# Attention, gated unit and soft mixture on one core: another order in the first pair of heads, the last slice by halves, normalisers and idle products moved

## The chip, the cores and the metric

The kernel runs on one core of one Trainium2 chip. A core has a matrix engine (TensorE, PE in the profile, with its weight loads as PEld), VectorE (DVE), ScalarE (ACT), GpSimd (POOL) and a queue for transfers (SyncE, SP). Each engine works through its own list of instructions in order; semaphores hold it where data are missing. The metric is the time of one execution on the device in microseconds, the median of several runs.

## The reference

```python
def _attn_ref(q, k, v):                       # q, k, v: 4 x 8 x 1152 x 64
    q_pool = q.reshape(B, H, S // 2, 2, D).mean(axis=3)
    scores = 1.0 / np.sqrt(D) * np.matmul(q_pool, k.transpose(0, 1, 3, 2))
    scores = scores - np.max(scores, axis=-1, keepdims=True)
    attn = np.exp(scores)
    attn = attn / (np.sum(attn, axis=-1, keepdims=True) + 1e-09)
    return np.matmul(attn, v)
def _moe_ref(x, w_gate, w_val, w_out):        # x: 2304 x 512, d_ff 1536
    g = x @ w_gate
    silu = g * (1.0 / (1.0 + np.exp(-g)))
    return silu * (x @ w_val) @ w_out
def _moe2_ref(x, phi, w1, w2):                # 8 experts of 4 slots
    logits = x @ phi
    d = np.exp(logits - logits.max(0, keepdims=True))
    d /= d.sum(0, keepdims=True) + 1e-09
    slot_input = (d.T @ x).reshape(E, S_per_e, D)
    for e in range(E):
        slot_out[e] = np.maximum(slot_input[e] @ w1[e], 0.0) @ w2[e]
    c = np.exp(logits - logits.max(1, keepdims=True))
    c /= c.sum(1, keepdims=True) + 1e-09
    return c @ slot_out.reshape(n_slots, D)
```

The pooled attention gives 4 x 576 tokens of 512 numbers; the gated unit (`_moe_ref`) works on them, and the soft mixture on its result.

## The kernel before

The work is written as one Python program; a scheduler with a timeline orders it per engine. What it keeps to: the program's order, priorities (`tc.high_priority`), the data, and the hand-made order marks `after` and `not_before`, which put an instruction behind a named one, or behind the last (or an earlier) exponential written so far.

*Attention* runs in 16 steps, one for each batch and pair of heads. Every number of 32 bits is split into a high and a low half of 16 bits, and products are made of the halves. `load_pair` loads a pair's keys, queries and values (`kr`, `qr`, `vr`); `split_pair` adds the two queries of a pool (`qr`, line 241), casts keys and queries to 16 bits (`kh`, `qh`), subtracts for the low halves (`kl`, `ql`), and copies the halves by transfers into the layouts that TensorE wants (`KK`, `QQ`, `KL`, `QH`, and `QD` for the maxima). The first pair has loads of its own for its first head (`first_split`).

Each pair's row maxima are computed one pair ahead: `row_max` multiplies `QD` and `kh` (`mx`, line 340) into a bank of PSUM, and VectorE reduces it (`mp`, lines 346 and 355; gathered in `nm`, line 358). The negated maxima go as a row `mt` by a transfer into `QH` (line 364), so that the second product of a score (`st`, line 421, "low score") subtracts the maximum. The first pair's own maxima come from `row_max_first` (products at line 291, reductions from line 301 on), head by head, the second head's while the first head's scores run.

A unit of a pair is one bank of scores: products at lines 420 and 421, the exponential on ScalarE (`P`, line 426), its low half `PL` on GpSimd (line 433), and later the products with V (`pv`). There are 21 units in a pair. Small constants are made in `selections`, at unit 20 of the program's first pair, on GpSimd: the identity in 16 bits `id16`, and the selection matrices `SEL`, `SELW` and `CN`.

*The gated unit* runs over 9 blocks of 256 tokens, each in 6 slices: products `g` and `v` (lines 691 to 696), tanh on ScalarE (line 702), two operations on VectorE (lines 703 and 705, the second multiplies by `v`), a cast to 16 bits (line 723), the low half (line 725), products for the mixture's logits `lp` (lines 735 and 740), which VectorE adds to `La` (line 746), and a transposing transfer. It fills the time from the fifth pair on.

*The mixture's end.* `block_end` gives a block's logits `L` (line 765), the running maximum, its correction `al` and the exponential `dT` (line 790); `block_turned` transposes it (`dt`, line 805) into `dS`, and `G` sums the tokens by slot. Behind the last `L` stand 30 products `warm` whose result nobody reads (line 771). `normalisers` turn the sums into factors `rn`, today folded into `CN`. After the last block `gt`, `si4p`, `siTp` and `hp` follow each other to the slots' inputs and the experts.

## Time and profile before

| | before |
|---|---|
| median of 3 runs | 897.52 us (895.04 to 897.69) |
| the profiled execution | 888.35 us, of it the span 886.6 |
| mean granted clock of TensorE | 0.973 |
| TensorE busy | 826.4 us |
| VectorE, ScalarE, GpSimd busy | 550.0, 366.3, 457.9 us |

The span is the time from the first to the last instruction of one profiled execution. A granted clock of 1.00 is 2.4 GHz, 0.50 is 1.2 GHz. In a row of a timeline the first number is the start in us, the second the length, then engine, line, operation, what it writes and reads, and in brackets the idle time of the engine before it and what ended it.

### The profile page before, as it was taken

The page shows a single profiled execution, that of the slowest core. Times are in us where ns is not written, and L with a number is a line of the kernel's source. Part 1 is how long each engine was busy: PE and PEld are TensorE (multiplying, and loading weights), DVE is VectorE, ACT ScalarE, POOL GpSimd, SP SyncE. Part 2 cuts the span into 40 slices and gives each one's busy share as a digit, 9 for nine tenths or more (in the row PEclk, how much of TensorE's full clock was granted, in tenths as well). Part 3 has the DMA queues.
Part 4 walks back from the last instruction along what each step waited for, and adds up shares of the span by engine and source line. Part 5 has one row for each costly group of instructions (what it writes and reads, how often), then busy time and mean ns, then how long its engine had stood idle before and what let it go on. Part 6 is the DMA issues. An engine that isn't in the chain of part 4 may idle for free.

```text
span 886.6 us, 23761 instructions
## 1 busy us (share of the span) xinstructions
PE 826.4 (93%) x9954; PEld 586.8 (66%) x9954; DVE 550.0 (62%) x1056; ACT 366.3 (41%) x690; POOL 457.9 (52%) x403
## 2 busy tenths in 40 slices
PE   5878898999888899999999999999999999997997
PEld 2545565677665567777776777777677777775445
DVE  5768777549787747585767767775744444444223
ACT  4545668578584633333333333333333212212112
POOL 8968669477888953655566365547345200000100
PEclk9989899899999989999999999999999999998998
DMA  6663847859588861454434171514112398457899
GB/s 193 172 163 79 264 134 218 244 152 264 138 246 226 230 173 25 102 108 97 101 81 118 32 177 32 120 30 85 33 25 37 113 307 271 84 164 189 283 280 287
DMA packets 154267, 134.69 MB, mean 152 GB/s; under 512 B 83632, under 2 KB 123120, under 8 KB 154160
## 3 DMA queue, kind: packets, MB, share of 16 engines
q1 hardware_dynamic: 152000, 133.13, 56.4%
q8 instruction: 78, 1.28, 0.6%
q10 hardware_dynamic: 2160, 0.04, 0.1%
q14 instruction: 29, 0.24, 0.1%
HBM read 84.10 MB, written 7.86 MB: 104 GB/s over the span
## 4 chain that ended last, share of the span: by engine, by line
PE 71%; DMA 11%; DVE 10%; issue 2%; SPq 2%; POOL 2%; ACT 2%; DVEq 0%; ACTq 0%; POOLq 0%
PE st L421 6%; PE st L420 6%; PE mx L340 5%; PE g L691 5%; PE g L696 5%; PE g L695 5%; PE v L691 5%; PE v L696 5%; PE v L695 4%; DMA qr<-in_qT 3%; PE pv L464 3%; PE pv L465 3%; PE pv L466 3%; DVE mp L346 3%; PE pv L456 2%
## 5 line engine op out<-in xcount | busy, mean ns | idle before, releaser
L433 POOL TENSOR_TENSOR PL<-P 128x512 f16<-128x512 f32 (+1 forms) x311 | 338.0, 1099 | 209.3 <-ACT P L426 205.8
L426 ACT ACTIVATE P<-st 128x512 f32<-128x512 f32 (+1 forms) x336 | 190.6, 580 | 249.2 <-PE st L421 205.8
L346 DVE TENSOR_REDUCE mp<-mx 128x1 f32<-128x512 f32 x270 | 179.0, 682 | 42.9 <-PE mx L340 41.3
L420 PE MATMUL st<-QQ,KK 128*128 128x512 f16 (+1 forms) x576 | 147.2, 292 | 6.4 <-ACT P L426 6.0
L421 PE MATMUL st<-QH,KL 65*128 65x512 f16 (+1 forms) x576 | 147.8, 295 | 4.6 <-DMA QH<-mt 2.8
L465 PE MATMUL pv<-VV,P 128*128 128x64 f16 x1088 | 141.2, 196 | 0.0
L464 PE MATMUL pv<-VV,P 128*128 128x65 f16 x1088 | 140.4, 195 | 0.5 <-DVE x L496 0.4
L466 PE MATMUL pv<-VV,PL 128*128 128x65 f16 x1088 | 139.0, 194 | 0.3 <-POOL PL L433 0.2
L691 PE MATMUL g<-xT,wgv 128*128 128x256 f16 x432 | 119.2, 276 | 4.1 <-DVE hs L703 3.4
L340 PE MATMUL mx<-kh,QD 128*128 128x512 f16 x270 | 105.5, 407 | 16.7 <-DVE mp L346 8.0
L464 PEld LDWEIGHTS <-P 128*128 128x128 bf16 x1088 | 105.7, 100 | 22.3 <-DVE x L496 3.4
L696 PE MATMUL g<-xT,wgv 128*128 128x256 f16 x432 | 119.0, 276 | 0.0
L695 PE MATMUL g<-xT,wgv 128*128 128x256 f16 x432 | 119.0, 275 | 0.0
L466 PEld LDWEIGHTS <-PL 128*128 128x128 f16 x1088 | 105.1, 100 | 20.7 <-issue 8.9
L696 PE MATMUL v<-xT,wgv 128*128 128x256 f16 x432 | 118.0, 273 | 0.0
L691 PE MATMUL v<-xT,wgv 128*128 128x256 f16 x432 | 118.0, 273 | 0.0
L695 PE MATMUL v<-xT,wgv 128*128 128x256 f16 x432 | 117.9, 273 | 0.0
L465 PEld LDWEIGHTS <-P 128*128 128x128 bf16 x1088 | 104.6, 99 | 10.3 <-issue 1.5
L691 PEld LDWEIGHTS <-wgv 128*128 128x128 f16 x864 | 85.3, 99 | 20.2 <-issue 2.7
L695 PEld LDWEIGHTS <-wgv 128*128 128x128 f16 x864 | 85.1, 98 | 17.4 <-issue 3.9
L696 PEld LDWEIGHTS <-wgv 128*128 128x128 f16 x864 | 85.1, 99 | 17.1 <-issue 0.8
L421 PEld LDWEIGHTS <-KL 65*128 65x128 f16 x576 | 52.1, 99 | 34.3 <-issue 13.2
(181 smaller groups left out, 1215.7 us busy)
## 6 DMA issues: line engine op xcount, KB each, us to landing
w<-in_w SPq DMA_DIRECT2D x16, 1024.0 KB, 7.4
w<-in_w SPq DMA_DIRECT2D x64, 256.0 KB, 5.5
vr<-in_vP SPq DMA_DIRECT2D x16, 585.0 KB, 5.3
KK<-kh SPq DMA_DIRECT2D x62, 144.0 KB, 2.9
qr<-in_qT SPq DMA_DIRECT2D x15, 576.0 KB, 4.8
kr<-in_kT SPq DMA_DIRECT2D x15, 576.0 KB, 4.4
r<-in_w_out SPq DMA_DIRECT2D x12, 512.0 KB, 4.4
r<-in_w_gate SPq DMA_DIRECT2D x24, 256.0 KB, 5.5
```

Of the source, the lines that this page charges most:

```text
L340: nc.tensor.matmul(t, q, kh[:, k0:k0 + kw], start=True, stop=True)
L346: nc.vector.reduce_max(out=mp[:, g, c:c + 1], in_=t, axis=AX.X)
L420: nc.tensor.matmul(t[:, o:o + w], KK[:, k], QQ[:, q0:q0 + w], start=True, stop=False)
L421: nc.tensor.matmul(t[:, o:o + w], KL[:, k], QH[:, q0:q0 + w], start=False, stop=True)
L426: marks.append(nc.scalar.activation(P32[:, :o], t[:, :o], AF.Exp, scale=1.0 / 16.0).ins.name)
L433: eng.tensor_tensor(out=PL[:, :o], in0=P32[:, :o], in1=PH[:, :o], op=ALU.subtract)
L464: nc.tensor.matmul(dst[:, :D + 1], PH[:, q], VV[:, c, 0, :], start=first, stop=False, skip_group_check=True)
L465: nc.tensor.matmul(dst[:, :D], PH[:, q], VV[:, c, 1, :D], start=False, stop=False, skip_group_check=True)
L466: nc.tensor.matmul(dst[:, :D + 1], PL[:, q], VV[:, c, 0, :], start=False, stop=(c == NCH - 1), skip_group_check=True)
L691: mm = nc.tensor.matmul(o, w[:, 0, d, f], xh, start=(d == 0), stop=False)
L695: nc.tensor.matmul(o, w[:, 0, d, f], xl, start=False, stop=False)
L696: nc.tensor.matmul(o, w[:, 1, d, f], xh, start=False, stop=(d == ND - 1))
```

## The change

Five edits. `selections` moves to the program's start, on GpSimd and with priority, and makes `CN` as a plain selection; both memsets of `KL` are VectorE's. The addition `qr` of the second pair is put behind a maximum of the first pair's second head, those of later pairs behind the fifth exponential from the last; the cast `kh` behind the transfer of the last `mt`. The last slice of the last block has its `v` in two half banks and is gated, cast, subtracted and multiplied by halves (`slice_last`). The exponential `dT` is written ahead of the copies of `al`, and `rn` multiplies when the slots' inputs are copied from `si4p`. The products without use come as 14 behind `L` and 16 behind `dt`.

```diff
+ADD_LEAD = 4
-WARM = 30
+WARM = [14, 16]
...
-    make_identity(nc, id32)
+    with tc.high_priority():
+        make_identity(nc, id32)
...
     def selections():
-        not_before(nc.gpsimd.tensor_copy(out=id16, in_=id32), 0)
         for z in range(P // NS):
             r = slice(z * NS, (z + 1) * NS)
-            not_before(nc.gpsimd.tensor_copy(out=SEL[r, :], in_=id32[r, r]), 0)
-            not_before(nc.gpsimd.tensor_scalar(SELW[r, :], id32[r, r], 1.0 / (HSC * W2SC), None, ALU.mult), 0)
-        not_before(nc.gpsimd.memset(CN, 0.0), 0)
+            nc.gpsimd.tensor_copy(out=SEL[r, :], in_=id32[r, r])
+        nc.gpsimd.tensor_scalar(SELW, SEL, 1.0 / (HSC * W2SC), None, ALU.mult)
+        nc.gpsimd.memset(CN, 0.0)
+        for z in range(2):
+            r = slice(z * P // 2, (z + 1) * P // 2)
+            nc.gpsimd.tensor_copy(out=CN[r, z, :], in_=SEL[r, :])
+        nc.gpsimd.tensor_copy(out=id16, in_=id32)
...
-    for t, eng in zip(KLs, (nc.vector, nc.gpsimd)):
-        eng.memset(t[D:D + 1, :, :], 16.0)
+    for t in KLs:
+        nc.vector.memset(t[D:D + 1, :, :], 16.0)
...
-        sub("a", b, p).tensor_tensor(out=qp, in0=qp, in1=qr[r, 1, :], op=ALU.add)
+        add = sub("a", b, p).tensor_tensor(out=qp, in0=qp, in1=qr[r, 1, :], op=ALU.add)
+
+        if (b, p) == steps[1]:
+            after(add, last_max[0])
+        elif not first:
+            not_before(add, ADD_LEAD)
...
-        cast("k", b, p, kh[r], kr[r])
+        k_cast = cast("k", b, p, kh[r], kr[r])
+        if mt_name:
+            after(k_cast, mt_name[-1])
...
+        last = j == NBLK - 1 and fp == NF // 2 - 1
         for a, nm in ((0, "g"), (1, "v")):
             tg, bf = ("st", STB) if j >= late and nm == "v" else ("mm", MMB)
-            t = ps(tg, [P, 2, BLK], bufs=bf, name=f"{nm}{j}_{fp}")
+            if last and nm == "v":
+
+                t = Halves(ps(tg, [P, BLK], bufs=bf, name=f"{nm}{j}_{fp}_{ci}") for ci in range(2))
+            else:
+                t = ps(tg, [P, 2, BLK], bufs=bf, name=f"{nm}{j}_{fp}")
...
+        if last:
+            for ci in range(2):
+                nc.vector.scalar_tensor_tensor(
+                    out=h[:, ci], in0=th[:, ci], scalar=SIL, in1=v[:, ci], op0=ALU.mult, op1=ALU.mult
+                )
+            stages.append(lambda: slice_last(j, fp, Hn, h, hs, hh))
+            return
...
+    def slice_last(j, fp, Hn, h, hs, hh):
+        t = ps("tr", [P, BLK], bufs=TRB, name=f"lp{j}_{fp}")
+        for ci in range(2):
+            w = W2S[:, 2 * fp + ci]
+            r = slice(ci * 2 * NS, (ci + 1) * 2 * NS)
+            nc.scalar.copy(hh[:, ci, :], h[:, ci])
+            nc.tensor.matmul(
+                t[r, :], w.rearrange("p a s -> p (a s)"), hh[:, ci, :], start=True, stop=False, skip_group_check=True
+            )
+            nc.vector.tensor_tensor(out=hs[:, 1, ci], in0=h[:, ci], in1=hh[:, ci, :], op=ALU.subtract)
+            nc.tensor.matmul(
+                t[ci * 2 * NS:ci * 2 * NS + NS, :], w[:, 0, :], hs[:, 1, ci, :], start=False, stop=True,
+                skip_group_check=True,
+            )
...
+        nc.vector.tensor_tensor(out=La, in0=La, in1=t, op=ALU.add)
...
-        for z in range(2):
-            r = slice(z * P // 2, (z + 1) * P // 2)
-            nc.vector.tensor_scalar(CN[r, z, :], SEL[r, :], rn[r, :], None, ALU.mult)
...
-    nc.vector.tensor_copy(out=si4[:, :DM // 2], in_=t[:, :DM // 2])
-    nc.scalar.copy(si4[:, DM // 2:], t[:, DM // 2:])
+    nc.vector.tensor_scalar(si4[:, :DM // 2], t[:, :DM // 2], rn, None, ALU.mult)
+    nc.scalar.activation(si4[:, DM // 2:], t[:, DM // 2:], AF.Copy, scale=rn)
```

What the scheduler makes of it, at three places. A name such as `qr_1_190` is tile `qr` of pair 1, counted from 0, with a buffer's number. First VectorE, behind the gathering of the first head's maxima (`nm_0`), where it reduces those of the second head (`mx_1_1` on). Before:

```order
L313 TENSOR_REDUCE nm_0_163<-mp_0_132 128x4
L241 TENSOR_TENSOR qr_1_190<-qr_1_190 128x576
L301 TENSOR_REDUCE mp_1_209<-mx_1_1_210 128x1
L301 TENSOR_REDUCE mp_1_209<-mx_1_2_220 128x1
L301 TENSOR_REDUCE mp_1_209<-mx_1_3_230 128x1
```

and of the change:

```order
L336 TENSOR_REDUCE nm_0_172<-mp_0_141 128x4
L324 TENSOR_REDUCE mp_1_218<-mx_1_1_219 128x1
L324 TENSOR_REDUCE mp_1_218<-mx_1_2_229 128x1
L324 TENSOR_REDUCE mp_1_218<-mx_1_3_239 128x1
L257 TENSOR_TENSOR qr_1_199<-qr_1_199 128x576
L324 TENSOR_REDUCE mp_1_218<-mx_1_4_278 128x1
```

The addition of the second pair's queries stands behind three maxima now. Next ScalarE at the end of the first pair, behind its last exponential. Before:

```order
L426 ACTIVATE P_0_20_732<-st_0_20_719 128x384
L195 CAST kh_2_755<-kr_2_285 128x1152
L327 ACTIVATE mt_1_736<-nm_1_705 128x9
L195 CAST VV_2_750<-vr_2_289 128x18x65
L364 DMA QH_1_243<-mt_1_736 1x128x9
L195 CAST qh_3_1342<-qr_3_948 128x576
L426 ACTIVATE P_1_0_746<-st_1_0_743 128x512
```

and of the change:

```order
L451 ACTIVATE P_0_20_731<-st_0_20_718 128x384
L350 ACTIVATE mt_1_735<-nm_1_704 128x9
L388 DMA QH_1_252<-mt_1_735 1x128x9
L211 CAST kh_2_754<-kr_2_294 128x1152
L211 CAST VV_2_749<-vr_2_298 128x18x65
L451 ACTIVATE P_1_0_745<-st_1_0_742 128x512
```

The third pair's `kh` has gone behind the transfer of `mt`, and the fourth pair's `qh` has left this place. Last, GpSimd at the start of the program, behind its memsets of `QD`, up to the first `PL`; of the change:

```order
L139 COPY SEL<-id_61 32x32 x4
L145 CAST id_66<-id_61 128x128
L144 COPY CN<-SEL 64x32
L140 TENSOR_SCALAR SELW<-SEL 128x32
L144 COPY CN<-SEL 64x32
L257 TENSOR_TENSOR qr_0_126<-qr_0_126 64x576
L238 TENSOR_TENSOR KL_101<-wgv_85,KK_0_131 64x1152
L237 TENSOR_TENSOR QQ_0_132<-wgv_84,QQ_0_132 64x576
L271 TENSOR_TENSOR ql_0_185<-qr_0_126,qh_0_183 64x576
```

Before, the first rows here were the subtractions for `KL` and `QQ`, with `qr_0` behind them, and the selections stood between the `PL`s of units 8 and 12.

## Rows read from the trace of the kernel before

**Rows 1.** The page, busy time of each engine over the span.
```profile
PE 826.4 (93%) x9954; PEld 586.8 (66%) x9954; DVE 550.0 (62%) x1056; ACT 366.3 (41%) x690; POOL 457.9 (52%) x403
```

**Rows 2.** Windows: length, then busy PE, PEld, DVE, ACT, POOL, then clock, DMA share, GB/s.
```profile
19.13:51.80 32.67, 27.44 (x372) 18.42 (x369) 25.40 (x43) 14.75 (x26) 27.22 (x31) 1.00 0.54 154
54.00:60.00 6.00, 4.07 (x11) 1.37 (x12) 3.24 (x5) 2.01 (x4) 4.70 (x4) 0.50 0.92 235
104.00:112.00 8.00, 7.14 (x35) 4.50 (x36) 6.47 (x12) 5.42 (x11) 4.40 (x5) 0.57 0.83 271
400.00:700.00 300.00, 296.88 (x3824) 219.98 (x3821) 192.56 (x374) 106.01 (x202) 164.02 (x142) 1.00 0.33 73
821.97:830.30 8.33, 7.08 (x82) 4.17 (x82) 2.97 (x10) 0.69 (x2) 0.52 (x1) 1.00 0.64 215
```

**Rows 3.** Waits of VectorE, 19 to 52 us: total, times, longest.
```profile
DVE qr L241 <- DMA qr<-in_qT: 8.6, 3, 5.8
```

**Rows 4.** Timeline of VectorE: start, length, line, operation, idle time before.
```profile
1.27 1.98 DVE L174 MEMSET KL<- 1x2304 f16 x1 [1.27 <-PEq L1208]
...
4.47 0.75 DVE L216 TENSOR_TENSOR wgv<-wgv 64x576 f32<-64x576 f32 x1 [1.22 <-DMA wgv<-in_qT]
...
19.13 1.22 DVE L241 TENSOR_TENSOR qr<-qr 128x576 f32<-128x576 f32 x1 [5.80 <-DMA qr<-in_qT]
...
51.60 0.18 DVE L358 TENSOR_REDUCE nm<-mp 128x9 f32<-128x27 f32 x1
```

**Rows 5.** Timeline of TensorE at four places.
```profile
17.69 0.63 PE L291 MATMUL mx<-KK,QQ 128*128 128x512 f16 x1
...
55.16 1.04 PE L340 MATMUL mx<-kh,QD 128*128 128x512 f16 x2 [3.24 <-DMA QD<-qh]
...
56.97 1.04 PE L421 MATMUL st<-QH,KL 65*128 65x512 f16 x2 [0.77 <-DMA QH<-mt]
...
104.86 1.04 PE L340 MATMUL mx<-kh,QD 128*128 128x512 f16 x2 [1.46 <-DMA QD<-qh]
...
235.05 0.59 PE L421 MATMUL st<-QH,KL 65*128 65x512 f16 x2 [2.07 <-DMA QH<-mt]
```

**Rows 6.** Timeline of ScalarE and its queue, 51 to 53 us.
```profile
51.19 1.15 ACT L195 CAST kh<-kr 128x1152 f16<-128x1152 f32 x1 [5.96 <-PE mx_r L340]
...
52.49 0.53 ACTq L364 DMA_DIRECT2D QH<-mt  x1
```

**Rows 7.** Tile mt, 45 to 110 us: issue to landing of its two transfers.
```profile
DMA to landing us min/median/max: 2.9/3.7/4.4
```

**Rows 8.** Groups of GpSimd, 18.6 to 47.4 us: busy us, mean ns.
```profile
L129 POOL TENSOR_SCALAR SELW<-id 32x32 f32<-32x32 f32 x4 | 1.1, 283 | 0.3
L128 POOL COPY SEL<-id 32x32 f32<-32x32 f32 x4 | 0.8, 203 | 0.1
```

**Rows 9.** Timeline of GpSimd, 6 to 20 us.
```profile
6.67 2.50 POOL L222 TENSOR_TENSOR KL<-wgv,KK 64x1152 f16<-64x1152 f32 x1 [2.07 <-DVE KK L218]
...
12.76 1.27 POOL L248 TENSOR_TENSOR ql<-qr,qh 64x576 f16<-64x576 f32 x1 [0.78 <-ACT qh L195]
...
18.70 2.55 POOL L433 TENSOR_TENSOR PL<-P 128x512 f16<-128x512 f32 x2
```

**Rows 10.** Timeline of all engines, 814 to 822 us.
```profile
814.54 0.68 DVE L705 SCALAR_TENSOR_TENSOR hs<-hs,v 128x512 f32<-128x512 f32 x1
...
815.26 0.62 ACT L723 CAST hs<-hs 128x512 bf16<-128x512 f32 x1 [3.37 <-DVE hs L705]
...
816.98 0.42 DVE L746 TENSOR_TENSOR La<-La,lp 128x256 f32<-128x256 f32 x1 [0.38 <-PE lp L740]
...
818.01 3.30 PE L771 MATMUL warm<-id 128*128 128x128 f16 x30
...
819.12 0.45 ACT L790 ACTIVATE dT<-L,ng 32x256 f32<-32x256 f32 x1
...
821.24 0.42 PE L805 MATMUL dt<-id,dT 32*128 32x32 f32 x2
```

More of the change, by code (lines that the diff above doesn't have):

```diff
@@ L37 @@
 SPLIT0 = 4
-SEL_U = 20
+PHI_U = 20
 ST_STEPS, ST_OF = 1, 3
@@ L61, with __init__, __getitem__ @@
 XB = 1
-WARM = 30
+WARM = [14, 16]
 MXB, STB, PVB, TRB, MMB = 2, 2, 1, 1, 2
+class Halves(list):
+    def __init__(self, ts):
+        super().__init__(ts)
+    def __getitem__(self, at):
+        return super().__getitem__(at[1] if isinstance(at, tuple) else at)
 @with_exitstack
@@ L167, in tile_pool_attention_glu_softmoe @@
     raw = {}
+    last_max = [None]
     QHs = {}
@@ L300, in row_max_first @@
                 t = scores(bank(), s, c * QT, QT)
-                nc.vector.reduce_max(out=mp[:, s, c:c + 1], in_=t, axis=AX.X)
+                last_max[0] = nc.vector.reduce_max(out=mp[:, s, c:c + 1], in_=t, axis=AX.X).ins.name
                 yield
@@ L329, in tile_pool_attention_glu_softmoe @@
     NGQ = SQ // D
+    mt_name = []
     has_max = {steps[0]}
@@ L362, in rest @@
             not_before(taken_off(mt, nm), 0)
-            nc.scalar.dma_start(out=QHs[b, p][D:D + 1].rearrange("o h (q g) -> o (h q) g", g=NGQ), in_=mt)
+            dma = nc.scalar.dma_start(out=QHs[b, p][D:D + 1].rearrange("o h (q g) -> o (h q) g", g=NGQ), in_=mt)
+            mt_name.append(dma.ins.name)
             has_max.add((b, p))
@@ L704, in block_slice @@
         h = th
-        nc.vector.scalar_tensor_tensor(out=h, in0=th, scalar=SIL, in1=v, op0=ALU.mult, op1=ALU.mult)
         hs = hs[:, :2 * QT].rearrange("p (a c n) -> p a c n", a=2, c=2)
         hh = hs[:, 0].bitcast(BF16)
+        if last:
[5 more added lines that the diff above has]
+            return
+        nc.vector.scalar_tensor_tensor(out=h, in0=th, scalar=SIL, in1=v, op0=ALU.mult, op1=ALU.mult)
         stages.append(lambda: slice_halves(j, fp, Hn, h, hs, hh))
@@ L728, in slice_halves @@
         ).ins.name
+    def slice_last(j, fp, Hn, h, hs, hh):
[12 more added lines that the diff above has]
+            )
+        moe["turn"] = nc.sync.dma_start_transpose(
+            out=Hn[:, fp].rearrange("p a c i f -> p (a c i) f"), in_=hs.rearrange("p a c n -> p (a c n)")
+        ).ins.name
+        nc.vector.tensor_tensor(out=La, in0=La, in1=t, op=ALU.add)
     def slice_logits(j, fp, hs, hh):
@@ L755, in normalisers, with warm @@
         nc.vector.tensor_copy(out=rn[2 * NS:, :], in_=rn[:2 * NS, :])
-        for z in range(2):
-            r = slice(z * P // 2, (z + 1) * P // 2)
-            nc.vector.tensor_scalar(CN[r, z, :], SEL[r, :], rn[r, :], None, ALU.mult)
+    def warm(i, mm):
+        w = ps("st", [P, P], bufs=STB, name="warm")
+        for _ in range(WARM[i]):
+            after(nc.tensor.matmul(w, id16, id16, start=True, stop=True), mm.ins.name)
     def block_end(j):
@@ L766, in block_end @@
         behind(mm)
-        if j == NBLK - 1 and WARM:
-            w = ps("st", [P, P], bufs=STB, name="warm")
-            for i in range(WARM):
-                after(nc.tensor.matmul(w, id16, id16, start=True, stop=True), mm.ins.name)
+        if j == NBLK - 1:
+            warm(0, mm)
         mb = mp.tile([NS, 1], F32, tag="mb", bufs=1, name=f"mb{j}")
@@ L781, in block_end @@
         nc.vector.tensor_scalar(ng, new, -1.0, None, ALU.mult)
+        dT = h_tile(f"dT{j}")[1][:NS, :BLK]
+        sb = mp.tile([NS, 1], F32, tag="sb", bufs=1, name=f"sb{j}")
         al = None
@@ L796, in block_end @@
             nc.vector.tensor_copy(out=s_run, in_=sb)
-        if j == NBLK - 1:
-            normalisers()
         stages.insert(0, lambda: block_turned(j, Hn, dT, al))
@@ L804, in block_turned @@
         for i in range(2):
-            behind(nc.tensor.transpose(t[:, i, :], dT[:, i * P:(i + 1) * P], id32[:NS, :NS]))
+            mm = nc.tensor.transpose(t[:, i, :], dT[:, i * P:(i + 1) * P], id32[:NS, :NS])
+            behind(mm)
+        if j == NBLK - 1:
+            warm(1, mm)
         dS = mp.tile([P, 2, 2, NS], F16, tag="dS", bufs=1, name=f"dS{j}")
@@ L913, in tile_pool_attention_glu_softmoe @@
     maxs = max_stream()
+    with tc.high_priority():
+        selections()
     first = first_load()
@@ L937, in moe_stream @@
                     yield False
-                for _ in block_slice(j, fp):
+                for k, _ in enumerate(block_slice(j, fp)):
                     stage()
+                    while stages and j == NBLK - 1 and fp == NF // 2 - 1 and k == 0:
+                        stage()
                     yield True
@@ L973, in tile_pool_attention_glu_softmoe @@
         for u, _ in enumerate(attn(b, p)):
-            if i == 0 and u == SEL_U:
-                selections()
+            if i == 0 and u == PHI_U:
                 nc.sync.dma_start(out=ph, in_=phi.rearrange("p (d s) -> p d s", d=ND))
@@ L1030, in tile_pool_attention_glu_softmoe @@
         )
+    normalisers()
     t = ps("mm", [P, DM], bufs=MMB, name="si4p")
```

5 lines of the change are left out of this document (2 added, 3 removed).

## The prediction

> **What bounds the kernel now.** I read the page first: TensorE is busy 93% of the span, no other compute engine over 62% [rows 1]. So only TensorE's idle time and its half-clock time can be won. The windows say where that lies: from 400 to 700 us TensorE is busy 296.9 of 300, from 19 to 52 only 27.4 of 32.7 [rows 2]. The first pair of heads, the step from it to the second pair, and the end are the places that this change can move much.
>
> Within the first pair the chain of waits runs through VectorE. It reduces the maxima of the second pair of heads while TensorE works on the first, and in the same queue stand the additions `qr` that pool the queries of later pairs, each waiting for a load. The view of VectorE's waits from 19 to 52 us has 8.6 us in three such waits [rows 3]; the largest, 5.8 us, ends at 19.13 us with the second pair's addition (1.22 us) [rows 4], and only then come the reductions of maxima that TensorE had issued at 17.69 [rows 5]. The other two waits share 2.8 us.
>
> At the step to the second pair TensorE runs out of products with V at 51.9 us and stands 3.24 us for the copies `QD` of the third pair's queries, and 0.77 us for the row `mt` of negated maxima in `QH` [rows 5]; the last maxima were gathered at 51.60 [rows 4]. Before `mt`, ScalarE casts `kh` at 51.19 for 1.15 us; `mt` goes out at 52.49 [rows 6] and lands 4.4 us later, the longer of its two landings between 45 and 110 us [rows 7]. From 54 to 60 us the granted clock is 0.50 [rows 2], that is 1.2 of 2.4 GHz, after TensorE stood idle.
>
> **The change part by part.**
>
> *Selections to the start.* They leave GpSimd's queue between the first pair's `PL`s: 1.1 + 0.8 us [rows 8], 1.9, and two small ones more, of which I count nothing. At the start they lie in the time before the first subtraction, `KL`, which waits 2.07 us for VectorE [rows 9]. But the first pair's `qr` now stands ahead of `KL` and has to wait for its load. The loads go out one behind another from the start, and I estimate the landing at 8.4 us, between 6.7 (where it would cost nothing, for `KL` starts there today) and 12 (where the order of today would wait for it). From `KL` to the first `PL` are 12.0 us, `qr` among them and a wait of 0.78 for ScalarE's cast of it [rows 9], which falls under `KL` now: 8.4 + 11.2 = 19.6 where 18.70 stands, +0.9, against −1.9 later. So GpSimd ends the first pair 1.0 earlier. VectorE's second memset is as wide as its first, 1.98 us from 1.27, and ends at 5.25; its next work starts at 4.47 today [rows 4], so +0.8 at most, and since that work itself waits for loads, I count 0.2.
>
> *`qr` behind the maxima.* VectorE starts the second head's reductions when TensorE has made them (18.2) instead of 20.3 (19.13 + 1.22): up to −2.1. The third pair's addition stands three maxima later and the fourth pair's leaves the stage, which takes most of the 2.8 us of waits away; the second pair's 1.22 stands between maxima now. VectorE is busy 25.4 of the 32.67 us from 19.13 to 51.80 [rows 2], so from 18.2 it could end at 43.6. TensorE has its own order of scores and maxima to keep, and GpSimd, whose `PL`s free the exponentials' buffers, is 1.0 earlier, no more; I put the gathered maximum at 47.0, nearer to VectorE's bound than to today: −4.6.
>
> *`kh` behind `mt`.* The 1.15 us cast is out of `mt`'s way: it is issued 0.6 us behind the gathered maximum, not 0.9 [rows 4, 6]. It needs 2.9 to 4.4 us to land [rows 7]: the first low score could come at 50.5 to 52.0. I take 52.5, since TensorE now holds 68 matmuls instead of 41 between its last maximum and that score, against 56.97 now [rows 5]. **−4.5** (−2.5, if the maximum comes at 49, to −6). Which landing `mt` gets depends on what else is moved: in 54 to 60 us the DMA share is 0.92 [rows 2]. The Trainium skill, "DMA: Bandwidth & Descriptors", section "Issuing engines are not separate DMA queues", has the transfers of all issuing engines run on the same 16 engines and interleave; by it `mt`, from ScalarE's queue, is late whenever SyncE's loads fall on it, as they do today, and the rows agree (4.4 us under load, 2.9 in the other case). By that rule alone, with the loads moving along with the pair, the sum would keep 4.4.
>
> *Later steps.* The additions now stand behind the fifth exponential from the end, so `QD` and `QH` of the next pair come later, and TensorE's order is another. I counted its matmuls between the last maximum of a pair and the next pair's first low score, and the time of their columns at 2.4 GHz: third pair 109 to 127 (5.5 to 4.9 us, and to the next maximum 1.7 to 5.9), fourth 213 to 145 (14.3 to 5.8, and 4.2 to 10.3), fifth 200 to 66 (14.1 to 2.5), ninth 110 to 107 (to the next maximum 1.6 to 6.6). A landing takes 2.9 to 4.4 us [rows 7]; where less is left as cover, the rest is a stall. Third pair: +1 (0 to 2), because `qr` of the fourth pair, in the first pair's stage today, now waits for the third's last maximum and has 5.9 us of cover, against its addition, a cast (1.2 and some 0.7) and the landing, 4.8 to 6.3, and whatever stands ahead of them. Fourth: −1.5, the length of the stall for `QD` at 104.86 [rows 5], which the new order covers. Fifth: +2 (0.4 to 1.9 for the landing alone, up to 2.7 with the wait for the maximum ahead of it). Ninth: −1 (0 to −2), half the stall for `mt` of 2.07 at 235.05 [rows 5], since its cover is as it was and only the cast has left `mt`'s way. Sum +0.5.
>
> *The last slice by halves.* Today VectorE's gating (0.68), ScalarE's cast (0.62) and VectorE's difference, as wide as the gating, follow each other from 814.54, and the sum `La` starts at 816.98 [rows 10]. Half widths I estimate at 0.40, 0.36 and 0.42, half plus some 0.06 each: 1.18, with 0.45 for the steps between and the product, gives 816.2: **−0.75** (0 to −0.9).
>
> *Products of no use.* 30 take 3.30 us from 818.01, and `dt`, whose input is ready at 819.57, comes at 821.24 [rows 10], 1.6 late. With 14 ahead it is not late, but 16 more, 1.74 us at the same 0.11, stand between it and `G`: 819.6 + 0.4 + 1.74 gives `G` at 821.8 instead of 821.97 (821.24, 0.42 and the step to `dS`): **−0.2** (−1 to +0.3). `al` behind the exponential and the normalisers out of `CN` are short operations beside that; the scaled copies of the slots' inputs are as wide as the plain ones; nothing for either. Tail: −1.0. From 821.97 to 830.30 the clock is 1.00 and TensorE busy 7.1 us [rows 2]. If it stayed at 0.50 for half of that work, the tail would take 3.5 more; that is a rival below. The Trainium skill, "TensorE: Matmul & The Clock Gate", section "What's actually happening", calls the throttled clock the default that activity releases; by that rule two lots with a wait between them could let it come back later than one lot does.
>
> **Sum.** −4.5 + 0.5 − 1.0 = −5.0 on the profiled execution's 888.35 us: 883.35. The runs shown have 897.5 as their median, 1.0% above the profiled one, so 897.52 x 883.35 / 888.35 = **892.5**. About 0.3%, 2.7 us, is what a measurement here can tell from no change: faster is under 894.8, slower over 900.2.
>
> **Rivals.**
> - *More gain.* The half clock behind the step goes as well, because the idle time before it is shorter. TensorE is busy 4.07 us of 54 to 60 at 0.50, so 2.0 are lost there: −7, 890.4; with the 3.1 at 104 to 112 (7.14 busy at 0.57) −10, 887.4 [rows 2]. For it: after the stall of 2.07 us two low scores take 0.59, full clock, after that of 3.24 and 0.77 they take 1.04. Against: two `mx` take 1.04 after only 1.46 [rows 5].
> - *Given back.* One new stall at the third or fifth pair with a fall of the clock, like that of 104 us, 1.46 + 3.1 = 4.6, leaves −0.4: 897.1. Or the clock comes back late in the tail: +3.5 leaves −1.5, 896.0. Or TensorE's order, not VectorE, holds the maxima, so that the change doesn't do what it says: the tail alone, −1.0, 896.5. For the last: VectorE has 7.3 us of idle time from 19 to 52, and only 2.8 of that is for `qr`.
> - *Slower.* Late additions make `QD` late. The addition of a pair's queries now waits near the end of the pair before it, then follow the cast `qh`, the transfer (2.9 to 4.4 us) and the first maximum; if that chain stands open it costs 4.6 each time with the clock. The gain of 5 is gone from 1.1 such stalls; two give +4.2, 901.8. For it: the fifth pair's cover falls from 14.1 to 2.5 us. Against: after 2.07 us at 235 the clock held, and from the fourth pair on TensorE has the gated unit's products to fill with.
>
> **How the numbers follow.** Forecast 0.50, more gain 0.12, given back 0.24 (stall 0.11, tail's clock 0.05, no effect 0.08), slower 0.14. So faster 0.62, same 0.24, slower 0.14. The range reaches to 887 in the one direction, both clocks of the first rival, and to 900 in the other, which leaves out the slower case and the far end of more gain, under 2 in 10. The forecast's own is 890 to 894.8 (head −2.5 to −6, later steps ±2, tail −0.3 to −1.6).
>
> **What would show it.** VectorE's 5.8 us wait for `qr` gone and its first reduction of the second head near 18.2; the second pair's maxima gathered by 47 and its first low score by 52.5, with `mt` issued under 0.7 us behind; GpSimd's first `PL` at 19.6; a stall of 1 to 3 us at the fifth pair; the last `La` near 1.7 us behind the start of the last gating; `dt` right behind its exponential. The prediction is wrong if the maxima stay at 50 or later, if a stall and a half clock stand at the third or fifth pair where there is none now, or if the clock in the 8 us of `G` to `siTp` is 0.50.

## The result, and the profile after

| | before | after |
|---|---|---|
| median | 896.28 us, 4 runs (893.19 to 897.69) | 885.78 us, 4 runs (884.15 to 887.45) |
| ratio | | 0.9888 (95%: 0.9850 to 0.9925) |
| the profiled execution | 888.35 us | 887.45 us |

The change is faster by 1.1%, some 10 us. The forecast was a gain of 5.0 us, 892.5 us, with a range from 887.0: the direction is right, the size half of what came, and the median lies 1.2 us outside the range.

The two profiled executions are only 0.9 us apart: the one of before was faster than all four of its timed runs, the one of after the slowest of its own. So a second profile of before (895.0 us of span, below) stands beside the first where longer stretches are compared. First the places that the prediction named, in the timeline of the changed kernel (start, length, engine, line, operation, idle time before):

```profile
8.61 1.39 POOL L257 TENSOR_TENSOR qr<-qr 64x576 f32<-64x576 f32 x1 [3.94 <-DMA qr<-in_qT]
...
17.58 1.99 DVE L324 TENSOR_REDUCE mp<-mx 128x1 f32<-128x512 f32 x3 [3.73 <-PE mx L314]
...
19.79 4.55 POOL L458 TENSOR_TENSOR PL<-P 128x512 f16<-128x512 f32 x4
...
47.19 0.18 DVE L382 TENSOR_REDUCE nm<-mp 128x9 f32<-128x27 f32 x1
...
47.65 0.53 ACTq L388 DMA_DIRECT2D QH<-mt  x1
...
50.68 0.65 PE L446 MATMUL st<-QH,KL 65*128 65x512 f16 x2 [2.01 <-DMA QH<-qh]
...
76.89 0.65 PE L364 MATMUL mx<-kh,QD 128*128 128x512 f16 x2 [0.86 <-DMA QD<-qh]
...
150.03 1.01 PE L446 MATMUL st<-QH,KL 65*128 65x512 f16 x2 [4.04 <-DMA QH<-mt]
...
266.27 1.01 PE L364 MATMUL mx<-kh,QD 128*128 128x512 f16 x2 [3.02 <-DVE kh L213]
```

In these rows the first pair goes as forecast: the first `PL` at 19.79 (19.6 was forecast), the maxima gathered at 47.19 (47.0), `mt` out 0.46 us behind them, the first low score at 50.68 (52.5), 6.3 us ahead of [rows 5]. Then come stalls that [rows 5] do not have: 4.04 us for `mt` at the fifth pair, where the forecast had a stall of 2, and 3.02 at the step to the eighth, for a cast `kh`. VectorE's waits for `qr` over the whole program (total, times, longest), in the kernel before and in the changed one:

```profile
DVE qr L241 <- DMA qr<-in_qT: 20.5, 10, 5.8
...
DVE qr L257 <- DMA qr<-in_qT: 0.6, 1, 0.6
```

The windows of the changed kernel around its stalls (columns as in [rows 2]):

```profile
48.00:62.00 14.00, 11.64 (x139) 6.61 (x134) 8.62 (x16) 8.53 (x14) 12.05 (x10) 0.88 0.94 230
98.00:114.00 16.00, 13.46 (x204) 10.33 (x202) 9.58 (x15) 11.74 (x23) 11.07 (x10) 0.79 0.22 67
146.00:154.00 8.00, 3.97 (x13) 1.64 (x14) 2.85 (x7) 3.47 (x6) 6.77 (x5) 0.57 0.92 238
```

and of the second profile of before:

```profile
48.00:62.00 14.00, 9.99 (x108) 5.31 (x104) 8.41 (x17) 5.92 (x10) 7.81 (x6) 0.76 0.70 199
98.00:114.00 16.00, 13.46 (x111) 8.14 (x110) 14.66 (x23) 10.53 (x21) 10.85 (x9) 0.79 0.71 211
```

The stretch at half clock at the second pair's step is shorter (mean clock 0.88 against 0.76), the one near 104 us is as long as before though the stall ahead of it is gone (0.79 in both), and one of 0.57 stands behind the fifth's stall. Over the whole span TensorE stands idle as long as before (65.3 us against 65.4 in the second profile of before); what is less is its busy time, 820.4 us against 829.6. The end of the program, in the timeline of the changed kernel:

```profile
812.46 0.41 DVE L739 SCALAR_TENSOR_TENSOR hs<-hs,v 128x256 f32<-128x256 f32 x1
...
814.13 0.42 DVE L784 TENSOR_TENSOR La<-La,lp 128x256 f32<-128x256 f32 x1 [0.36 <-PE lp L777]
...
815.16 1.24 PE L817 MATMUL warm<-id 128*128 128x128 f16 x14
...
816.87 0.42 PE L860 MATMUL dt<-id,dT 32*128 32x32 f32 x2 [0.46 <-ACT dT L844]
...
817.22 1.89 PE L817 MATMUL warm<-id 128*128 128x128 f16 x16
...
819.03 2.11 PE L885 MATMUL G<-Hn,dS 128*32 128x256 bf16 x36
...
821.10 2.21 PE L1086 MATMUL gt<-CN,G_acc 128*128 128x64 f32 x12
```

From the last gating to `La` are 1.67 us where [rows 10] have 2.44, −0.77. `dt` is no longer late. But `G` takes 2.11 us and `gt` 2.21, against 1.17 and 1.55 in the kernel before; the granted clock from 819.03 to 827 us is 0.78 here, and 1.00 from 821.97 to 830.30 in [rows 2]. In this execution the late clock took back 0.94 + 0.66 = 1.6 us, more than the halves gave.

### The profile page after: what moved, and what is told of

Read it like the earlier page. It is cut to its first block, busy times and chain, and to the rows that moved or that the text cites. A ratio compares the mean times of both kernels' runs of the same rounds, so it can differ in the third digit from the quotient of the medians.

```text
span 885.7 us, 23738 instructions
## 1 busy us (share of the span) xinstructions
PE 820.4 (93%) x9954; PEld 583.7 (66%) x9954; DVE 556.6 (63%) x1057; ACT 366.8 (41%) x691; POOL 450.7 (51%) x401
## 4 chain that ended last, share of the span: by engine, by line
PE 72%; DVE 12%; DMA 7%; issue 3%; ACT 3%; POOL 2%; SPq 1%; ACTq 0%; DVEq 0%; POOLq 0%
PE st L446 7%; PE st L445 6%; PE mx L364 6%; PE g L721 5%; PE g L726 5%; PE g L725 5%; PE v L721 5%; PE v L726 5%; PE v L725 5%; DVE mp L370 4%; PE pv L489 3%; PE pv L490 3%; PE pv L491 3%; DMA r<-in_w_val 2%; PE hp L1155 2%
## 5 line engine op out<-in xcount | busy, mean ns | idle before, releaser
L370 DVE TENSOR_REDUCE mp<-mx 128x1 f32<-128x512 f32 x270 | 179.6, 683 | 52.5 <-PE mx L364 50.6
L489 PE MATMUL pv<-VV,P 128*128 128x65 f16 x1088 | 138.0, 194 | 2.9 <-DVE x L521 2.9
L490 PE MATMUL pv<-VV,P 128*128 128x64 f16 x1088 | 138.8, 196 | 0.6 <-POOL VV L292 0.6
L490 PEld LDWEIGHTS <-P 128*128 128x128 bf16 x1088 | 103.6, 98 | 12.6 <-issue 4.3
L446 PEld LDWEIGHTS <-KL 65*128 65x128 f16 x576 | 52.7, 100 | 35.4 <-issue 13.5
```

Of the source, the lines that this page charges most:

```text
L370: nc.vector.reduce_max(out=mp[:, g, c:c + 1], in_=t, axis=AX.X)
L446: nc.tensor.matmul(t[:, o:o + w], KL[:, k], QH[:, q0:q0 + w], start=False, stop=True)
L489: nc.tensor.matmul(dst[:, :D + 1], PH[:, q], VV[:, c, 0, :], start=first, stop=False, skip_group_check=True)
L490: nc.tensor.matmul(dst[:, :D], PH[:, q], VV[:, c, 1, :D], start=False, stop=False, skip_group_check=True)
```

## The experiments

Every run was timed in 5 rounds against the kernel before on the same chip. The table has all of them; under it stand the edits, one by one. "Idle" is the profile's span less TensorE's busy time; "half" is 2 x (1 − mean granted clock) x span, the time at 1.2 GHz (from a clock of three digits, so good to about 1 us); the waits are those of VectorE for the loads of `qr` and of the products `st` for `mt`, all in us. "Lead" is `ADD_LEAD`, 4 in the change: the addition stands behind the fifth exponential from the last.

| kernel | ratio (95%) | span | idle | half | `qr` | `mt` |
|---|---|---|---|---|---|---|
| before, first profile | | 886.6 | 60.2 | 48 | 20.5 | 2.8 |
| before again | 1.0005 (0.9983–1.0027) | 895.0 | 65.4 | 55 | 19.4 | 4.6 |
| the change | 0.9888 (0.9850–0.9925) | 885.7 | 65.3 | 50 | 0.6 | 5.5 |
| the change, old end | 0.9897 (0.9871–0.9923) | 882.4 | 67.0 | 39 | 0.2 | 5.8 |
| before, new end | 1.0004 (0.9980–1.0028) | 895.5 | 65.4 | 61 | 19.5 | 3.4 |
| before + selections | 1.0015 (0.9988–1.0041) | 892.9 | 67.0 | 43 | 18.9 | 3.5 |
| before + cast's mark | 1.0065 (1.0038–1.0092) | 897.8 | 70.0 | 56 | 12.2 | 5.5 |
| before + additions' marks | 1.0002 (0.9976–1.0029) | 896.0 | 68.4 | 70 | 0 | 9.4 |
| before + all marks | 0.9846 (0.9806–0.9885) | 880.4 | 63.0 | 39 | 0 | 2.0 |
| the same, new end | 0.9888 (0.9848–0.9927) | 885.2 | 61.4 | 55 | 0 | 2.3 |
| before + cast's + later marks | 0.9896 (0.9855–0.9937) | 881.8 | 63.6 | 48 | 6.4 | 4.0 |
| the change, no mark on `qr` | 0.9915 (0.9885–0.9945) | 883.0 | 61.0 | 39 | 17.5 | 4.7 |
| the same, old end | 0.9950 (0.9922–0.9979) | 887.9 | 67.3 | 44 | 19.5 | 5.1 |
| the change, later marks only | 0.9897 (0.9861–0.9933) | 882.0 | 64.4 | 37 | 6.6 | 8.2 |
| the change, second pair's mark only | 1.0031 (1.0000–1.0061) | 902.4 | 78.7 | 56 | 15.7 | 11.5 |
| the change, no cast's mark | 1.0101 (1.0064–1.0138) | 902.3 | 73.8 | 63 | 1.2 | 10.8 |
| the change, lead 12 | 0.9783 (0.9743–0.9823) | 871.4 | 52.7 | 30 | 0 | 2.8 |
| the change, lead 20 | 0.9819 (0.9771–0.9867) | 870.6 | 54.9 | 24 | 0 | 5.7 |
| before + cast's + later marks, lead 12 | 0.9913 (0.9881–0.9944) | 884.1 | 67.4 | 35 | 7.4 | 9.0 |
| the change, lead 12, no cast's mark | 0.9914 (0.9872–0.9956) | 882.4 | 64.8 | 37 | 1.4 | 3.1 |

**Before again.** No edit.

> The kernel of before once more, for a second profile: its first one took 888.4 us where the median was 896 to 898. Theory A (the change's gain lies in the first pair of heads and its step): the extra 8 us of a typical execution are in stalls and half clock between 50 and 310 us, at the steps of the pairs, and the maxima of the second pair are still gathered at 51 to 52 us. Theory B (the gain is in the later steps, which the other order happens to fit better): the same, but with the extra stalls at steps that the change leaves without one. Time 896, ratio 1.000 within 0.3%.

Median 895.96. Its maxima of the second pair are gathered at 51.84, so the first pair of before is steady from one execution to the other (51.60 in [rows 4]); the stalls at the steps are there again:

```profile
54.98 1.04 PE L340 MATMUL mx<-kh,QD 128*128 128x512 f16 x2 [2.83 <-DMA QD<-qh]
...
104.47 0.68 PE L340 MATMUL mx<-kh,QD 128*128 128x512 f16 x2 [2.13 <-DMA QD<-qh]
```

It is 8 us longer than the first profile: the first four transfers of `mt` are issued at most 0.9 us apart in the two, all from the fifth on 3 to 5 us later, and 4 us more lie behind the last of them. One profile of such a kernel says little about 5 us.

**The end apart from the rest.** The changed end on the lists of before (the copies for `CN` on GpSimd, late), and the end of before on the lists of the change.

```diff
+        last = j == NBLK - 1 and fp == NF // 2 - 1
...
-WARM = 30
+WARM = [14, 16]
```

> The order of before up to the last slices, with the changed end alone: the last slice by halves, the normalisers at the slots' inputs, 14 and 16 products of no use. If the end is worth what its two terms say, -0.75 and -0.2, and the clock comes back late for G and gt as the changed kernel's profile shows (+1.3 there): -1 to +0.5 us, ratio 0.999 to 1.0005. If most of the change's -10.5 comes from the end: ratio 0.992 or less.

> The order of the change up to the last slices, with the end of before: one slice of full width, factors in CN, 30 products behind L. Theory A and B both have the gain in the order of the attention: -9 to -10.5 us, ratio 0.988 to 0.990, with the second pair's maxima gathered at 47 us in the profile. If the end carried it: ratio 0.996 or more.

1.0004 and 0.9897 (the change: 0.9888). The whole gain is in the order of the attention; the end is worth nothing that 0.25% can show. The new end's clock is not always late: with the same 14 and 16 products `G` took 1.17 us in the profiles of all nine other kernels with this end, among them the one without marks on `qr`, whose TensorE timeline reads

```profile
816.21 0.96 PE L813 MATMUL warm<-id 128*128 128x128 f16 x14
...
818.15 1.07 PE L813 MATMUL warm<-id 128*128 128x128 f16 x16
819.15 1.17 PE L881 MATMUL G<-Hn,dS 128*32 128x256 bf16 x36
```

**No marks on the additions.**

```diff
-        if (b, p) == steps[1]:
-            after(add, last_max[0])
-        elif not first:
-            not_before(add, ADD_LEAD)
```

> The change without its two marks on the addition of the queries (qr), so that VectorE meets the second pair's addition first again and waits for its load near 19 us. Theory A: the maxima of the second pair are gathered 3 to 4 us later than in the change (50 to 51 us) and the time is 4 to 5 us above the change's, ratio to before 0.993. Theory B: the order of the later steps changes too, so anything from 0.988 to 1.00, and the milestones of the first pair don't tell the time.

0.9915: 0.3% above the change, which the intervals don't tell apart. Theory A's first half came (maxima at 52.67, later still than it had them). Its second half, 0.993, lies within the interval (0.9885 to 0.9945), so this run alone doesn't settle it; but a kernel without the first pair's lead is still 0.85% faster than before. The run that settles more is the one without the second pair's mark alone, below.

**One part at a time, on the kernel before.** Four kernels: the cast's mark, the two marks on the additions, the selections with the memset, and both kinds of mark together.

```diff
+        if mt_name:
+            after(k_cast, mt_name[-1])
```

> The kernel of before with one mark more: the cast kh stands behind the transfer of the last mt, in every pair. Theory A (the prediction's: it only clears mt's way at the step to the second pair): -0.3 to -1 us, ratio 0.999. Theory C (it pays at every step, because mt and the copies of the halves come before the 1.15 us cast): mt of the pairs 2 to 6 earlier by 1 to 2 us each, -4 to -6 us by the end, ratio 0.994 to 0.996.

```diff
+        if (b, p) == steps[1]:
+            after(add, last_max[0])
+        elif not first:
+            not_before(add, ADD_LEAD)
```

> The kernel of before with the two marks on the addition of the queries alone. Theory A: the second pair's maxima are gathered at about 48 us instead of 51.7 and the time is 3.5 to 4.5 us less, ratio 0.995 to 0.996. Theory C: the same early maxima, but the lead is spent by the sixth pair, within 2 us of before, ratio 0.998 to 1.002.

```diff
+    with tc.high_priority():
+        selections()
...
+    for t in KLs:
+        nc.vector.memset(t[D:D + 1, :, :], 16.0)
```

> The kernel of before with the selections at the start of GpSimd's list and both memsets on VectorE. Theory A: GpSimd's first PL at 19.8, its end of the first pair 1 us earlier, the maxima of the second pair within 1 us of before: -0.5 to -1 us, ratio 0.999. Theory C has no other price for it alone: 0 to -2.

> Both marks together, the addition and the cast, without the selections' move and with the end of before. Theory A: -4.5 to -6 us, ratio 0.993 to 0.995, maxima of the second pair gathered by 48. Theory C: as much as the cast's mark alone and at most 2 us more, ratio 0.992 to 0.995. If the selections are what is missing to the change's 0.9897, this stays at 0.995 or above.

1.0065, 1.0002, 1.0015, and 0.9846 together: no part gives anything alone (the cast's mark costs 0.65%), the two kinds of mark together give all that the change gives or more. For the sum of the marks theory A and theory C both fall; for the additions' marks alone theory C's range was met (1.0002, within 0.998 to 1.002). What each mark does is in the profiles. Without the additions' marks, VectorE stands at an addition of a later pair whose load hasn't come, and the gated unit's operation behind it in the list stands too; around 323 us in the second profile of before:

```profile
323.46 0.76 DVE L241 TENSOR_TENSOR qr<-qr 128x576 f32<-128x576 f32 x1 [4.72 <-DMA qr<-in_qT]
...
325.21 0.28 PE L691 MATMUL g<-xT,wgv 128*128 128x256 f16 x1 [1.73 <-DVE hs L703]
```

and around 327 us in that of the kernel "before, new end", whose lists up to the last slices are those of before but for a few rows:

```profile
327.06 0.76 DVE L253 TENSOR_TENSOR qr<-qr 128x576 f32<-128x576 f32 x1 [4.11 <-DMA qr<-in_qT]
...
328.07 0.68 DVE L723 SCALAR_TENSOR_TENSOR hs<-hs,g 128x512 f32<-128x512 f32 x1
...
328.81 0.40 PE L711 MATMUL g<-xT,wgv 128*128 128x256 f16 x1 [6.19 <-DVE hs L723]
```

What such a wait of VectorE costs TensorE differs from one execution to another: behind 4.14 us in the first profile of before TensorE stands 0.57 us, behind 4.72 in the second 1.73, behind 4.11 here 6.19, the most of the three. The issues of `mt` show what this stage is worth. There are 15 of them. In the four profiles with neither kind of mark the eighth stands at 303 to 310 us and the tenth at 410 to 420; in the six with the cast's mark and the later pairs' marks at lead 4 they stand at 301 to 303 and 404 to 407. Of a mean gain of 9.5 us at the fifteenth issue, 4.7 are there at the eighth, 5.5 come between the eighth and the tenth, where this wait stands, and none behind it. From the eighth to the tenth issue, in the second profile of before and in the change (columns as in [rows 2]):

```profile
306.90:414.40 107.50, 103.04 (x1246) 75.04 (x1243) 65.79 (x129) 35.32 (x69) 60.03 (x51) 0.97 0.42 100
301.90:405.40 103.50, 101.53 (x1235) 74.00 (x1233) 70.78 (x131) 35.78 (x69) 60.59 (x51) 0.98 0.41 98
```

TensorE's idle time there falls from 4.5 to 2.0 us. The waits for `qr` can't be the whole of it: with the additions' marks alone none is left, and the stage still takes 107.9 us (302.9 to 410.8), at a mean clock of 0.95.

With the additions' marks and without the cast's, `kh` is cast ahead of the last maximum, its copies `KK` go out with `mt`, and `mt` lands 5.1 us after its issue. Around 557 us, additions' marks alone:

```profile
555.66 0.74 DVE L199 CAST kh<-kr 128x1152 f16<-128x1152 f32 x1
...
555.68 0.54 SPq L189 DMA_DIRECT2D qr<-in_qT  x1
...
557.02 0.16 DVE L365 TENSOR_REDUCE nm<-mp 128x9 f32<-128x27 f32 x1
...
557.38 0.46 SPq L264 DMA_DIRECT2D KK<-kh  x1
...
557.47 0.48 ACTq L371 DMA_DIRECT2D QH<-mt  x1
...
562.68 0.38 PE L428 MATMUL st<-QH,KL 65*128 65x512 f16 x1 [3.05 <-DMA QH<-mt]
```

and the same place with both marks, where TensorE has no stall for `mt`:

```profile
546.39 0.54 SPq L189 DMA_DIRECT2D qr<-in_qT  x1
...
546.81 0.16 DVE L368 TENSOR_REDUCE nm<-mp 128x9 f32<-128x27 f32 x1
...
547.02 0.76 DVE L199 CAST kh<-kr 128x1152 f16<-128x1152 f32 x1
...
547.25 0.48 ACTq L374 DMA_DIRECT2D QH<-mt  x1
...
548.47 0.46 SPq L266 DMA_DIRECT2D KK<-kh  x1
```

`mt` comes from ScalarE's queue, and it is late when SyncE's transfers run beside it: from 300 us on its longest landing is 5.1 us with the additions' marks alone and 4.3 with both kinds, the median 3.2 and 2.9. The Trainium skill, "DMA: Bandwidth & Descriptors", section "Issuing engines are not separate DMA queues", on which the prediction drew, has the transfers of all issuing engines run on the same 16 engines and interleave; these rows agree. But the copies `KK` aren't all of it. With both kinds of mark they go out 1.2 us behind `mt`, and `mt` still lands in 4.2 us here, where it takes 2.9 in the second profile of before and 2.8 at lead 12. In both kernels above the 576 KB load `qr` is issued 0.9 to 1.8 us ahead of `mt`; `qr` has one buffer, so a later addition also makes the next load late. Between the two landings lie only 0.9 us, and why the stall of 3.05 us is gone with both marks isn't shown beyond that.

**Which of the marks.** The change with the later pairs' marks alone, with the second pair's alone, and without the cast's; and both marks with the changed end.

```diff
-        if (b, p) == steps[1]:
-            after(add, last_max[0])
-        elif not first:
+        if not first and (b, p) != steps[1]:
             not_before(add, ADD_LEAD)
```

> The change without the mark on the second pair's addition alone; the later pairs' additions stay behind their exponentials, and all other lists are as in the change but for a few rows. It prices the step of the prediction that it gave the largest gain, VectorE's first wait. Theory A: the maxima of the second pair are gathered 2 to 4 us later (49 to 51 us) and the time is that much longer, ratio 0.992 to 0.994. Theory D (the gain lies in the later additions, which no longer stand in VectorE's list waiting for loads): the first wait returns, but what it delays is caught up by the third pair: within 1.5 us of the change, ratio 0.988 to 0.991.

```diff
-        elif not first:
-            not_before(add, ADD_LEAD)
```

> The change with the second pair's mark alone: the later pairs' additions stand where the scheduler puts them, as before. Theory A: most of the gain stays, ratio 0.990 to 0.992. Theory D: VectorE waits for the loads of later qr again (some 15 us in all, against 0.6), the gated unit's products wait behind it near 320 us, and the time is 3 to 8 us above the change's, ratio 0.992 to 0.998.

```diff
-        if mt_name:
-            after(k_cast, mt_name[-1])
```

> The change without the mark that puts the cast kh behind the transfer of the last mt. Theory A: 0.5 to 1 us above the change, ratio 0.989 to 0.991. Theory D with both marks needed: TensorE's waits for mt rise from 5.5 to 9 us or more, as with the addition's marks alone, and most of the gain goes, ratio 0.996 to 1.000.

```diff
-    with tc.high_priority():
-        selections()
...
             if i == 0 and u == PHI_U:
+                selections()
```

> Both marks and the changed end, with the selections and the memset where they were before: the order of the two marks alone up to the last slices. Theory D: as the two marks alone, 0.9846, less 0 to 1 us for the end: 0.983 to 0.986, below the change's 0.989. If the marks' 0.9846 was luck of one order on one chip: 0.988 to 0.990.

0.9897, 1.0031, 1.0101, 0.9888. The second and the third came out above every range that was named for them (0.990 to 0.998, 0.989 to 1.000): taking out one of these marks costs all that the change had gained, or more. The fourth fell into the range named for the case that 0.9846 was luck of one order. The first is the cleanest of all, since its lists are those of the change but for a few rows. VectorE's first wait is back, the maxima are gathered 3.1 us later, and by the fifth pair both kernels stand at the same stall; its timeline:

```profile
20.49 0.76 DVE L257 TENSOR_TENSOR qr<-qr 128x576 f32<-128x576 f32 x1 [6.64 <-DMA qr<-in_qT]
...
50.30 0.18 DVE L380 TENSOR_REDUCE nm<-mp 128x9 f32<-128x27 f32 x1
...
152.14 1.01 PE L444 MATMUL st<-QH,KL 65*128 65x512 f16 x2 [3.67 <-DMA QH<-mt]
```

3.1 us at the second pair, 2.1 at the fifth (152.14 against 150.03), 0.2 at the eighth issue of `mt` (302.1 against 301.9), nothing measurable at the end. With the second pair's mark alone the 5.9 us wait for `qr` stands in front of the gated unit again, and TensorE idles 11.2 us in four waits for it:

```profile
DVE qr L257 <- DMA qr<-in_qT: 15.7, 9, 5.9
...
PE g L719 <- DVE hs L731: 11.2, 4, 5.5
```

**The two marks alone, and their distance.** On the kernel before: cast's mark and later marks, all else untouched. Then the change with the later additions 13 exponentials back instead of 5, and the order without marks on `qr` once more, with the end of before.

```diff
-ADD_LEAD = 4
+ADD_LEAD = 12
```

> The kernel of before with two marks alone: the cast kh behind the last mt, and the additions from the third pair on behind their exponentials. The second pair's addition, the selections, the memset and the end are those of before. Theory D (these two marks are the whole gain): ratio 0.984 to 0.990, VectorE's waits for qr down to the first one, 6 us. If the first mark, the selections or the end are needed beside them: 0.993 or above.

> The change with the later additions behind the 13th exponential from the last instead of the 5th, so earlier in VectorE's list. Theory D (what counts is that the load of qr has landed when VectorE comes to the addition): VectorE waits for qr again, 3 to 12 us in all, and the time lies between the change and the kernel with the second pair's mark alone, ratio 0.991 to 1.002. If any mark behind an exponential does it, whatever the distance: 0.987 to 0.991, with no wait for qr.

> The change without its two marks on the addition, as an earlier run, now with the end of before: the same lists up to the last slices, so the same 0.9915 within 0.4% if that was the order's and not the chip's. Theory D has no place for a gain here, since VectorE waits 17.5 us for qr with this order: it must be that these waits fall where TensorE has other work, above all no wait of the gated unit's products near 320 us. Else 0.997 to 1.001.

0.9896, 0.9783, 0.9950. Two marks alone reach the change's gain. The second expectation was wrong in sign: at 13 exponentials no wait for `qr` came back, so at 5 the addition was later than its load needed, and what hangs on it (`qh`, its copies, the next maxima, the next load) was late as well. That this is what gains the further 1.1% isn't shown, since a quarter or more of the rows of TensorE, VectorE and ScalarE stand in another order. The stall of 4 us at the fifth pair is gone. From the page:

```profile
PE 818.7 (94%) x9954; PEld 580.8 (67%) x9954; DVE 551.1 (63%) x1057; ACT 364.9 (42%) x691; POOL 454.7 (52%) x401
...
PEclk9999999999979999999999999999999999999998
```

But for its last slice, the clock row has a single slice below 9. The third kernel repeats an order that gained 0.85% and now gains 0.5% (0.22 to 0.78): smaller, but still a gain without a single mark on `qr`, and with 19.5 us of waits for it.

**How far, and with what else.** Distances of 13 on the kernel before with two marks, 13 without the cast's mark, and 21.

> The kernel of before with the cast's mark and the later additions 13 exponentials back; second pair's addition, selections and end as before. Theory E (the later mark must keep the addition behind its load, but no later than that, because the cast qh, the copies QD and QH and the next pair's maxima hang on it): ratio 0.976 to 0.984, VectorE without waits for qr but the first, TensorE at half clock for 20 us or less up to 650 us. If the selections or the second pair's mark are needed for the 0.978: 0.985 to 0.992.

> The change with the later additions 13 exponentials back and without the cast's mark. Theory E: with the additions earlier there is more room for mt and the copies, so the cast's mark is worth less than the 2 per cent it was at 5 exponentials: ratio 0.982 to 0.995, TensorE's waits for mt 5 to 9 us against 2.8. If the cast's mark is needed in any case: 0.998 to 1.010.

> The change with the later additions behind the 21st exponential from the last, that is, a whole pair back. Theory E: at that distance the mark no longer keeps the addition behind its load: VectorE waits for qr again, 4 us or more in all, and the time goes up from 0.978 to 0.985 or more. If the loads land earlier than that: no wait for qr, 0.975 to 0.982.

0.9913, 0.9914, 0.9819. The first missed theory E's range and fell into the other one: with the two marks alone 13 exponentials give no more than 5 (0.9913 against 0.9896). At 21 the wait for `qr` still doesn't come back, against the expectation: the loads land earlier than that. Taking out the cast's mark costs 2% at 5 and 1.3% at 13. At 5 TensorE's waits for `mt` go from 5.5 to 10.8 us with it, but at 13 only from 2.8 to 3.1, where 5 to 9 were expected; what the mark is worth there doesn't come through `mt`. The 0.9783 needs more than the two marks: without the second pair's mark, the selections' move and the new end, which were worth nothing at 5, it is 0.9913.

## Where the prediction was right and where it failed

*The first pair.* Each event came within some 2 us of its forecast: `qr` loaded by 8.6 (8.4), first `PL`, VectorE's first reduction at 17.58 (18.2), the maxima, `mt`. The −4.5 us at the second pair's first low score was −6.3. But the step "`qr` behind the maxima" took this for a gain of the whole program. It is not: with the second pair's mark taken out the maxima came 3.1 us later and the time stayed (0.9897 against 0.9888, each ±0.4%, so that 3 or 4 us can't be excluded by the times alone). In the profiles the lead is spent at later steps: at the fifth pair both kernels stand and wait for `mt`, and at the eighth they are level.

*The later steps* are the term that failed, and with it the path: the prediction had nearly the whole gain in the first pair's lead, and the runs have it in the marks of the later pairs. They stood in the sum with +0.5, four estimates from the cover that TensorE's order left. Their signs were partly right: the stall at 104 us went, the third pair's came (0.86, forecast 1), the fifth's came (4.04 with half clock, forecast 2). What the term left out is that the same edit takes the waits for `qr` out of VectorE's list in every pair, 20 us in ten waits, of which the prediction read only the three up to 52 us, and that the cast's mark works in every pair, not at the first step alone. The two marks together, without anything else of the change, measure −1.04% (0.9855 to 0.9937), or −9 us, against +0.5 in the sum; the larger part of it comes between the eighth and the tenth `mt`, for which the term has only the ninth pair's −1. One of the prediction's own signs of being wrong stands in the profile too, the stall with half clock at the fifth pair, and its rival "given back" priced it at 4.6 us, nearly the whole gain; the change gained twice the forecast all the same. So the right direction owes something to luck: the reason given for it, the first pair's lead, isn't what gained. (The stall of 2.07 us at 235.05, which the prediction put at the ninth pair, is the seventh's; it is gone, as 1 of its 2 us were forecast to be.)

*Half clock.* The rival "more gain" had the time at −7 to −10 with a chance of 0.12, since shorter stalls would shorten the stretches at 1.2 GHz at 54 and at 104 us as well. The median is −10, but only a part of this mechanism came: the first of the two stretches is shorter, the second is not. Work at 1.2 GHz takes up to twice as long (`G` 2.11 us against 1.17), so the time there, 50 us in the changed kernel's profile against 55 in the second of before, accounts for some 3 of the 9.3 us between the spans at most; with the old end it was 39 us, some 8 of 12.6. What the rest of TensorE's shorter busy time is, isn't settled.

*The end.* −0.75 for the halves (−0.77 in the profile) and −0.2 for the two lots (`L` to `G` 4.42 us against 4.52) were right as sizes; the rival of the late clock, priced at +3.5, came at +1.6 in one profile and at nothing in the nine others with this end. Together the end measures nothing.

*What stays open.* The order without marks on `qr` gained 0.5 to 0.85%, and with the second pair's mark added the scheduler's lists differ in every engine and 0.3% were lost. How far an order as such moves the time is seen best at the cast's mark: alone it gives 1.0065, with the selections' move beside it, which by itself gives 1.0015, it gives 0.9950 ("no mark on `qr`", old end). So over 1% can hang on what else stands in the lists, as much as the change gained. For the two marks speaks that all six kernels with both at lead 4 lie at 0.9846 to 0.9897, and all six with one kind alone at 0.9915 to 1.0101. But the six with both are only two orders with small variations (the change, its old end and "later marks only" share one; "before + all marks", its new end and "before + cast's + later" the other), so luck of an order isn't excluded. A run that takes only the waits for `qr` away and leaves all other rows where they were is missing, and why the small edits pay only together with the longer distance is not settled either.

## What to carry to other kernels

An operation that waits for a load in an in-order list can cost what stands behind it, so look for such waits over the whole program and not only where they are longest. Then try several places for the operation: behind its load, but not much later, for what it feeds is late too (in the whole change 5 exponentials gave 1.1%, 13 gave 2.2%, 21 gave 1.8%; with two marks alone 5 and 13 gave the same). A lead won at an early stage is worth only what the next bottleneck leaves of it: take the edit out of the changed kernel before believing its price. Where a scheduler makes another order of the whole program out of one mark, one pair of kernels doesn't price the mark: measure it beside several others. For a small transfer that the next stage waits for, see which large ones are issued just before it, on whatever queue (landing 2.8 to 2.9 us here without one, 4.2 to 5.1 with one).

## What the runs showed of the hardware

Stalls of about the same length came with half clock in some places and not in another: those of 2.83 us at 54.98 and 2.13 at 104.47 in the second profile of before did (0.76 from 48 to 62 us, 0.79 from 98 to 114), the 2.07 us at 235.05 in [rows 5] did not (1.00 from 231 to 245). In the end of the program the 30 products took 3.30 us, mostly at half clock, in the first profile of before and 1.85 in that of the change with the old end (1.2 and 2.4 GHz), so that `G` began 4.52 us after `L` in the one and 2.95 in the other: what idle products are worth differs from run to run by more than their order does.
